# Token weights of a wave mixer flipped as bf16 instead of f32

## The chip, the cores and the metric

The kernel runs on one core of one Trainium2 chip. A core has a matrix engine (TensorE, PE in the profile; PEld is its weight load), three engines that work on 128 partitions by columns (VectorE = DVE, ScalarE = ACT, GpSimd = POOL) and SyncE (SP), which here only issues transfers. Each engine runs its own list of instructions strictly in order and waits on semaphores for the others. SBUF is the on-chip memory; PSUM, where TensorE writes, has eight banks of 2 KB per partition. The metric is device time in microseconds.

## What is computed

An attention with a decaying state, then a mixing network on its output:

```
for t in range(S):                       # r, k, v: [4, 8, 768, 48]
    cur = einsum('bhd,bhe->bhde', u * k_t, v_t)
    y_t = einsum('bhd,bhde->bhe', r_t, state + cur)
    state = w * state + einsum('bhd,bhe->bhde', k_t, v_t)
x = y as [4, 768, 384]                   # heads side by side
theta = x @ w_theta
zr, zi = x * cos(theta), x * sin(theta)
un = x + einsum('ts,bsd->btd', w_tok_r, zr) + einsum('ts,bsd->btd', w_tok_i, zi)
out = un + max(un @ w_ch, 0)
```

All inputs and the output are f32. The two token weights, `w_tok_r` and `w_tok_i`, are 768 x 768 and serve all four batches.

## The kernel before

The 768 positions of a batch are six chunks of 128, worked on in three pairs of chunks. For each batch, `heads` (line 487) scales r by powers of w (Rw, on POOL) and flips it (RT). For each pair, `attention` (line 506) loads k and v, scales k (Kw, POOL), flips it (KT), casts v (vb, ACT), computes scores (line 543), masks them (mAT, DVE, line 548), carries the state on (Sb), and sums the outputs in PSUM (lines 627 and 632). The diagonal term goes another way: PD (DVE), a small matmul, dg, yd (POOL). Then x is formed (DVE, line 639), flipped (xT), multiplied by w_theta (line 651), and sine and cosine (ACT, lines 655 and 658) lead to zi (POOL) and zr (DVE). `mixing` (line 668) needs zr and zi of all three pairs of a batch: for each of six row blocks, 12 matmuls of 128 x 384 (line 683) against WrT and WiT, then un (DVE), its flip (uT), the channel matmul (line 700), fin (DVE, line 704) and a store (SP, line 708). The mixing of one batch runs beside the attention of the next.

WrT and WiT are the token weights turned over, made once by `token_weights` (line 445): twelve row blocks of 128 x 768, each loaded in f32 into one of ten load buffers (`ld`, which k, v, w_theta and w_ch use in turn as well), turned over by six 128 x 128 transposes on TensorE against the f32 identity `ident_f`, and copied out of PSUM as bf16. All other flips go through `flips` (line 468), where the source is bf16 already, the identity is `ident`, and six or eight blocks fill one bank.

The order of all work is fixed when the kernel is built. Every piece is a task with the engines it may run on, an assumed cost on each, what it reads and writes, a priority, and the PSUM places it takes; `P.order()` (line 88) plays these costs through and writes each engine's list. PSUM is cut into six places, two of two banks and four of one (`SLOTS`, line 23); scores, score outputs, theta and channel sums take a double place, and so did a flipped row block of the token weights. Loads go out on SP in the order in which the program text asks for them, each when its buffer is free by the plan; stores go ahead of loads as soon as fin is ready by the plan (line 710). SP waits in order, so a load behind a store waits for what the store waits for. A task with several engines (`ev` at line 482: ACT or DVE) goes to the one that the plan finds free sooner. `lock=True` keeps the plan from running two such tasks at once: Rw, Kw, PD, yd and zi have it.

The change touches lines 445 to 466. Those of lines outside it that the text goes back to:

```
    Ls = ring(NL, [C, 2, H, Dp], F32, "ld")                      # ten load buffers
    load(3500 / parts, r_fs[b % NR][:, h], ...)                  # a batch's r: 1152 KB
    P.add({SP: (1000, 2000)}, ... out ..., prio=-2e6)            # the stores
```

Of the kernel before, what the change touches and what calls it, by code (L numbers as in the profile page):

```python
# [16 lines left out]
BF16 = mybir.dt.bfloat16  # L17
# [3 lines left out]
PE, DVE, ACT, POOL, SP = "PE", "DVE", "ACT", "POOL", "SP"  # L21
# [167 lines left out]
def act_op(n, psum=True, ptr=False):  # L189
    return (n / 1.2 + (85 if psum else 100) + (90 if ptr else 0), 135)  # L190


def dve_op(n, rate=1.0):
    return (n / (0.96 * rate) + 70, 115)


def pool_op(n, rate=1.8):
    return (170 + rate * n, 100)


def pe_op(ns):
    return (ns, 215)
# [24 lines left out]
def build(ctx, tc, nc, r, k, v, w, u, moe_w_theta, moe_w_tok_r, moe_w_tok_i, moe_w_ch, out):  # L227
    B, H, S, D = r.shape
    HD = H * D
    C = 128  # L230
    NCH = S // C
# [8 lines left out]
    P = Plan(SLOTS)  # L240
    banks = [ps.tile([C, n, 512], F32, name=f"bank{i}") for i, n in enumerate(SLOTS)]

    def dbl(tok):
        return banks[P.bank_of[tok]]
# [4 lines left out]
    def bank16(tok):  # L249
        return banks[P.bank_of[tok]].bitcast(BF16)[:, 0]  # L250

    def ring(n, shape, dt, nm):
        return [sb.tile(shape, dt, name=f"{nm}{i}") for i in range(n)]
# [3 lines left out]
    def copy(e, dst, src):  # L257
        if e == ACT:
            nc.scalar.activation(dst, src, Act.Copy)  # L259
        else:  # L260
            eng_of[e].tensor_copy(dst, src)  # L261

    ident_f = sb.tile([C, C], F32, name="ident_f")
    ident = sb.tile([C, C], BF16, name="ident")
# [18 lines left out]
    Ls = ring(NL, [C, 2, H, Dp], F32, "ld")  # L283
# [116 lines left out]
    def load(ns, dst, src, wr, pos=None):  # L400
        if pos is None:
            nload[0] += 1
            pos = nload[0]
        P.add({SP: (ns, 2100)}, lambda e: nc.sync.dma_start(out=dst, in_=src), wr=wr,  # L404
              prio=-1e6 + pos, name="load")
# [11 lines left out]
    def slot():  # L417
        nslot[0] += 1
        return nslot[0] % NL
# [9 lines left out]
    def flat(i):  # L429
        return Ls[i].rearrange("p a h d -> p (a h d)")  # L430

    def L2(i):
        return [("L", i, 0), ("L", i, 1)]
# [11 lines left out]
    def token_weights(tos, prio):  # L445
        for to in tos:
            for src, dst, key in ((moe_w_tok_r, WrT, "WrT"), (moe_w_tok_i, WiT, "WiT")):
                i = slot()
                load(1100, flat(i)[:, :S], src[to * C:(to + 1) * C, :], L2(i))
                tok = ("W", key, to)  # L450

                def flip(e, i=i, tok=tok):
                    for g in range(2):
                        for j in range(3):
                            o = (3 * g + j) * C
                            nc.tensor.matmul(dbl(tok)[:, g, j * C:(j + 1) * C],  # L456
                                             flat(i)[:, o:o + C], ident_f, is_transpose=True,
                                             start=(j == 0), stop=(j == 2))
                P.add({PE: pe_op(660)}, flip, rd=L2(i) + ["ident_f"], acq=[(tok, 2)],
                      prio=prio + to, name="Wflip")  # L460

                def evac(e, tok=tok, dst=dst, to=to):
                    copy(e, dst[:, :, to * C:(to + 1) * C].rearrange("p (g j) c -> p g j c", g=2),
                         dbl(tok)[:, :, :3 * C].rearrange("p g (j c) -> p g j c", j=3))
                P.add({ACT: act_op(6 * C), DVE: dve_op(6 * C)}, evac, use=[tok],
                      wr=[(key, to)], prio=prio + to, name="Wevac")

    def flips(dst, blocks, tok, prio, rd, wr, name, opts, src=lambda t: t):
        n = len(blocks)
# [12 lines left out]
    def ev(n):  # L482
        return {ACT: act_op(n), DVE: dve_op(n, 2.0)}
# [233 lines left out]
    attention(0, 1, 15)  # L717
    attention(0, 2, 25)
    token_weights(range(0, 3), 40)
    load_r(1)  # L720
    heads(1, 100)
    token_weights(range(3, NCH), 40)
    square(moe_w_ch, Wch, "Wch", 46)
    for b in range(1, B + 1):
# [39 lines left out]
```

## Time and profile before

| | |
|---|---|
| five runs | 158.66, 158.07, 158.57, 158.22, 161.15 us |
| median | 158.57 us |
| the profiled execution | 158.66 us, of which the span of its instructions is 156.8 us |
| TensorE busy | 131.9 us of the span |
| DVE, ACT, POOL busy | 110.2, 76.2, 75.6 us |
| moved by DMA | 25.0 MB |
| f32 flips of the token weights (line 456) | 72, from 29.9 to 48.3 us |
| copies out of them | 9 on ACT, 3 on DVE, from 30.9 to 49.1 us |
| first mixing matmul | 42.06 us |
| last load landed | 93.8 us |

Busy time of an engine is the union of its instructions. Matmuls overlap in the pipeline, so a group's mean duration is longer than its pace: 326 ns is the mean of a mixing matmul, and three of them move the chain on by 0.49 us. The chain of waits is read from the end backwards: each piece is the work or the transfer that the next piece waited for.

### The profile page before, as it was taken

The page shows a single profiled execution, that of the slowest core. Times are in us where ns is not written, and L with a number is a line of the kernel's source. Part 1 is how long each engine was busy: PE and PEld are TensorE (multiplying, and loading weights), DVE is VectorE, ACT ScalarE, POOL GpSimd, SP SyncE. Part 2 cuts the span into 40 slices and gives each one's busy share as a digit, 9 for nine tenths or more (in the row PEclk, how much of TensorE's full clock was granted, in tenths as well). Part 3 has the DMA queues.
Part 4 walks back from the last instruction along what each step waited for, and adds up shares of the span by engine and source line. Part 5 has one row for each costly group of instructions (what it writes and reads, how often), then busy time and mean ns, then how long its engine had stood idle before and what let it go on. Part 6 is the DMA issues. An engine that isn't in the chain of part 4 may idle for free.

```text
span 156.8 us, 3653 instructions
## 1 busy us (share of the span) xinstructions
PE 131.9 (84%) x1491; PEld 92.6 (59%) x1491; DVE 110.2 (70%) x158; ACT 76.2 (49%) x119; POOL 75.6 (48%) x61
## 2 busy tenths in 40 slices
PE   4077586569899999999989969999999999999950
PEld 1056464457687666668756737678567676566620
DVE  6296799840723989987999867658996975545540
ACT  3977228349887446648844365615418354000000
POOL 7000730759995755966599976900712343100000
PEclk9999999999999999999999999999999999999996
DMA  4999999999899999999999950311300022022022
GB/s 152 264 224 187 163 266 394 366 397 367 265 187 156 166 209 186 167 164 250 293 176 210 152 95 0 104 49 51 104 0 4 0 102 104 0 100 81 19 100 100
DMA packets 59962, 25.00 MB, mean 159 GB/s; under 512 B 50473, under 2 KB 58410, under 8 KB 59946
## 3 DMA queue, kind: packets, MB, share of 16 engines
q1 hardware_dynamic: 59920, 24.78, 74.1%
q8 instruction: 11, 0.18, 0.6%
q14 instruction: 5, 0.04, 0.1%
q10 hardware_dynamic: 26, 0.00, 0.0%
HBM read 20.06 MB, written 4.72 MB: 158 GB/s over the span
## 4 chain that ended last, share of the span: by engine, by line
PE 47%; DMA 18%; DVE 13%; SPq 8%; POOL 7%; issue 3%; ACT 2%; ACTq 1%; POOLq 0%; DVEq 0%
PE bank L683 20%; DMA ld<-in_k_dram 7%; SPq L404 7%; PE bank L473 7%; DMA r_f<-in_r_dram 7%; PE bank L700 7%; POOL Rw L492 4%; PE bank L651 3%; DMA ld<-in_v_dram 3%; PE bank L456 3%; POOL Kw L520 2%; DVE PD L553 2%; DVE fin L704 2%; DVE zr L661 2%; PE bank L543 2%
## 5 line engine op out<-in xcount | busy, mean ns | idle before, releaser
L683 PE MATMUL bank<-zi,WiT 128*128 128x384 bf16 x144 | 29.6, 326 | 0.0
L683 PE MATMUL bank<-zr,WrT 128*128 128x384 bf16 x144 | 29.1, 326 | 0.0
L548 DVE TENSOR_TENSOR mAT<-bank,mask 128x1024 bf16<-128x1024 f32 x24 | 28.7, 1215 | 0.1
L520 POOL TENSOR_TENSOR Kw<-ld,wpinv 128x768 bf16<-128x768 f32 x10 | 18.6, 1860 | 19.2 <-DMA ld<-in_k_dram 19.2
L664 POOL TENSOR_TENSOR zi<-x,sin 128x768 bf16<-128x768 bf16 x12 | 20.6, 1717 | 14.8 <-ACT sin L655 14.8
L568 POOL TENSOR_TENSOR yd<-dg,vb 128x768 bf16<-128x768 f32 x12 | 17.6, 1476 | 20.3 <-ACT dg L259 16.0
L689 DVE TENSOR_TENSOR un<-bank,x 128x384 bf16<-128x384 f32 x24 | 13.3, 552 | 6.7 <-PE bank L683 6.7
L492 POOL TENSOR_TENSOR Rw<-r_f,wpow 128x576 bf16<-128x576 f32 x12 | 16.6, 1405 | 2.9 <-DMA r_f<-in_r_dram 2.9
L683 PEld LDWEIGHTS <-WiT 128*128 128x128 bf16 x144 | 12.9, 98 | 7.1
L683 PEld LDWEIGHTS <-WrT 128*128 128x128 bf16 x144 | 12.8, 97 | 7.0
L259 ACT ACTIVATE vb<-ld 128x768 bf16<-128x768 f32 x12 | 10.1, 845 | 13.5 <-DMA ld<-in_v_dram 13.5
L639 DVE TENSOR_TENSOR x<-bank,yd 128x768 bf16<-128x768 f32 x12 | 11.4, 953 | 6.9 <-PE bank L632 4.8
L651 PE MATMUL bank<-Wth,xT 128*128 128x384 bf16 x72 | 13.7, 326 | 3.1 <-DVE xT L261 1.5
L704 DVE SCALAR_TENSOR_TENSOR fin<-bank,un 128x768 f32<-128x768 f32 x12 | 11.5, 956 | 6.3 <-PE bank L700 6.3
L259 ACT ACTIVATE RT<-bank 128x768 bf16<-128x768 bf16 x16 | 12.0, 814 | 5.4 <-PE bank L473 5.4
L655 ACT ACTIVATE sin<-bank 128x768 bf16<-128x768 f32 x12 | 9.7, 811 | 9.9 <-DVE fin L704 4.8
L700 PE MATMUL bank<-Wch,uT 128*128 128x384 bf16 x72 | 13.7, 326 | 0.7 <-DVE uT L261 0.7
L661 DVE TENSOR_TENSOR zr<-bank,x 128x768 bf16<-128x768 f32 x12 | 11.4, 950 | 3.0 <-ACT bank L658 3.0
L543 PE MATMUL bank<-RT,KT 64*128 64x128 bf16 x192 | 9.8, 229 | 2.1 <-ACT KT L259 0.6
L651 PEld LDWEIGHTS <-xT 128*128 128x128 bf16 x72 | 6.9, 97 | 7.9 <-DVE xT L261 1.9
L473 PE MATMUL bank<-ident,Rw 128*128 128x128 bf16 x96 | 8.3, 242 | 3.8 <-POOL Rw L492 2.0
L658 ACT ACTIVATE bank<-bank,pi 128x768 f32<-128x768 f32 x12 | 10.5, 873 | 0.0
(79 smaller groups left out, 209.8 us busy)
## 6 DMA issues: line engine op xcount, KB each, us to landing
ld<-in_k_dram SPq DMA_DIRECT2D x24, 192.0 KB, 5.7
ld<-in_v_dram SPq DMA_DIRECT2D x24, 192.0 KB, 5.3
out_dram<-fin SPq DMA_DIRECT2D x12, 384.0 KB, 2.5
r_f<-in_r_dram SPq DMA_DIRECT2D x3, 1152.0 KB, 10.1
ld<-in_moe_w_tok_r_dram SPq DMA_DIRECT2D x6, 384.0 KB, 7.5
ld<-in_moe_w_tok_i_dram SPq DMA_DIRECT2D x6, 384.0 KB, 8.5
r_f<-in_r_dram SPq DMA_DIRECT2D x2, 576.0 KB, 4.5
ld<-in_moe_w_theta_dram SPq DMA_DIRECT2D x1, 384.0 KB, 5.0
```

The lines of the kernel that those rows point to most:

```text
L259: nc.scalar.activation(dst, src, Act.Copy)
L473: nc.tensor.matmul(bank16(tok)[:, i * C:(i + 1) * C], s, ident, is_transpose=True, start=(i == 0), stop=(i == n - 1))
L492: eng_of[e].tensor_mul(Rw[:, :, 2 * hp:2 * hp + 2, :D].transpose([0, 2, 1, 3]), rf[:, 2 * hp:2 * hp + 2, :].rearrange("p h (n d) -> p h n ...
L520: eng_of[e].tensor_mul(Kw[:, :, :, :D].rearrange("p a h d -> p (a h) d"), Ls[ik][:, :, :, :D].rearrange("p a h d -> p (a h) d"), wpinv.rea ...
L548: P.add({DVE: dve_op(8 * C)}, lambda e, tk=tk, c=c: nc.vector.tensor_mul(mAT[:, c].rearrange("p a h t -> p (a h) t"), dbl(tk).rearrange("p ...
L568: P.add({POOL: pool_op(2 * HD, 1.7)}, lambda e: nc.gpsimd.tensor_mul(yd.rearrange("p a (h d) -> p (a h) d", h=H), wide(dg, D), vb.rearrang ...
L651: nc.tensor.matmul(dbl(th)[:, t, :HD], xT[:, ND * t + dk, :], Wth[:, dk, :], start=(dk == 0), stop=(dk == ND - 1))
L661: P.add({DVE: dve_op(2 * HD)}, lambda e: nc.vector.tensor_mul(zr[:, 2 * pr:2 * pr + 2], dbl(th)[:, :, :HD], x[:, 2 * pr:2 * pr + 2]), use= ...
L664: P.add({POOL: pool_op(2 * HD, 1.9)}, lambda e: nc.gpsimd.tensor_mul(zi[:, 2 * pr:2 * pr + 2], x[:, 2 * pr:2 * pr + 2], sn), rd=xk + [("si ...
L683: nc.tensor.matmul(bank(tm)[:, :HD], WT[:, so, to * C:(to + 1) * C], z[:, so], start=(part == 0 and j == 0), stop=(part == 3 and j == 2))
L700: nc.tensor.matmul(dbl(tf)[:, t, :HD], uT[:, ND * t + dk, :], Wch[:, dk, :], start=(dk == 0), stop=(dk == ND - 1))
L704: P.add({DVE: dve_op(2 * HD)}, lambda e: nc.vector.scalar_tensor_tensor(fin, dbl(tf)[:, :, :HD], 0.0, un, op0=Alu.max, op1=Alu.add), use=[ ...
```

## The change

The row block is cast to bf16 in its own load buffer, in two halves, each written over the first half of the bytes that it is read from. The planner may put this cast on ACT, DVE or POOL. The six transposes then read bf16 against the bf16 identity, and write bf16 into one bank instead of f32 into two; the copy out reads bf16 from one bank. The costs that the planner assumes change with it (660 to 340 ns for the flip).

```diff
-                def flip(e, i=i, tok=tok):
-                    for g in range(2):
-                        for j in range(3):
-                            o = (3 * g + j) * C
-                            nc.tensor.matmul(dbl(tok)[:, g, j * C:(j + 1) * C],
-                                             flat(i)[:, o:o + C], ident_f, is_transpose=True,
-                                             start=(j == 0), stop=(j == 2))
-                P.add({PE: pe_op(660)}, flip, rd=L2(i) + ["ident_f"], acq=[(tok, 2)],
+                half = Ls[i].bitcast(BF16).rearrange("p a h d -> p (a h d)")[:, :2 * S] \
+                    .rearrange("p (g c) -> p g c", g=2)[:, :, :S // 2]
+                P.add({ACT: act_op(S, False), DVE: dve_op(S, 2.0), POOL: pool_op(S, 1.1)},
+                      lambda e, i=i, half=half: copy(
+                          e, half, flat(i)[:, :S].rearrange("p (g c) -> p g c", g=2)), rd=L2(i), wr=L2(i),
+                      prio=prio + to, name="Wcast")
+
+                def flip(e, half=half, tok=tok):
+                    for j in range(NCH):
+                        nc.tensor.matmul(bank16(tok)[:, j * C:(j + 1) * C],
+                                         half[:, j // 3, (j % 3) * C:(j % 3 + 1) * C], ident, is_transpose=True,
+                                         start=(j == 0), stop=(j == NCH - 1))
+                P.add({PE: pe_op(340)}, flip, rd=L2(i) + ["ident"], acq=[(tok, 1)],
                       prio=prio + to, name="Wflip")
 
                 def evac(e, tok=tok, dst=dst, to=to):
-                    copy(e, dst[:, :, to * C:(to + 1) * C].rearrange("p (g j) c -> p g j c", g=2),
-                         dbl(tok)[:, :, :3 * C].rearrange("p g (j c) -> p g j c", j=3))
-                P.add({ACT: act_op(6 * C), DVE: dve_op(6 * C)}, evac, use=[tok],
-                      wr=[(key, to)], prio=prio + to, name="Wevac")
+                    copy(e, dst[:, :, to * C:(to + 1) * C],
+                         bank16(tok)[:, :S].rearrange("p (j c) -> p j c", j=NCH))
+                P.add(ev(S), evac, use=[tok], wr=[(key, to)], prio=prio + to, name="Wevac")
```

Since the plan is made anew from these tasks, instructions outside these lines move too, on every engine. The new cast has no `lock`.

## The prediction

> **What bounds the kernel now.** I read the slices first, then the chain that ended last, then the timeline of the engines where the chain turns from loads to TensorE.
>
> ```profile
> PE   4077586569899999999989969999999999999950
> PEclk9999999999999999999999999999999999999996
> DMA  4999999999899999999999950311300022022022
> GB/s 152 264 224 187 163 266 394 366 397 367 265 187 156 166 209 186 167 164 250 293 176 210 152 95 0 104 49 51 104 0 4 0 102 104 0 100 81 19 100 100
> ```
>
> A slice is 3.92 us. Loads run without a pause until 93 us: near 380 GB/s from 24 to 41 us (token weights and two loads of r, long rows), near 163 GB/s while k and v come in. Then they stop and TensorE works alone, with its clock full, so no term below needs a clock. The two stages meet here:
>
> ```profile
> 82.51 1.47 SPq L404
> 83.98 0.05 issue
> 84.03 4.96 DMA ld<-in_v_dram
> 89.09 0.06 ACT vb L259
> 89.16 0.81 issue
> 89.96 0.81 ACT sin L655
> 90.77 0.78 ACT bank L658
> 91.57 0.96 DVE zr L661
> 92.53 0.47 DVE xT L261
> 93.05 1.15 PE bank L651 x6
> ```
>
> A v load lands, ACT casts it (vb) and only then reaches the sine and cosine queued behind; zr, xT and theta (L651) follow. TensorE waited 1.53 us for that theta. From the last score output of batch 2 (L627 and L632, 94.69) to TensorE's end (152.29) are 57.6 us. The work queued there, by the chain's pieces (three mixing matmuls 0.49, six theta or channel matmuls 0.97, six flips 0.34): 180 mixing 29.3, thirteen theta and channel groups 12.6, sixteen flip groups 5.4, batch 3's attention 7.6, these outputs 0.7; together 55.6. So the end is this meeting point plus TensorE's remaining work, and the loads set the meeting point.
>
> **Flips: -4.1 us of TensorE.** The chain gives 12 f32 flips 1.33 to 1.40 us, 0.113 each; bf16 flips take 0.34 for six, 0.057 each. 72 of them: 8.2 becomes 4.1. Six of the twelve groups (4.1 us in f32) stand between the first mixing matmul (42.06) and 49.4, when 21 mixing matmuls are done (3.4); in the new order all flips stand before the first.
>
> **Copies out: -1.8 us off the path.** Before, nine on ACT at 0.81 and three on DVE at 0.958: 10.2. After, the planner places seven on ACT (0.81, as for bf16 xT) and five on DVE (0.547, as for xT): 8.4. Both engines have idle time there, so this counts as nothing by itself; without that cover it is 1.8 us.
>
> **Casts: twelve new instructions.** The planner puts four on ACT, six on DVE, two on POOL. ACT: 0.845, the row of vb (same shape and types). DVE:
>
> ```profile
> L345 DVE CAST ident<-ident_f 128x128 bf16<-128x128 f32 x1 | 0.2, 220 | 0.0
> L261 DVE COPY xT<-bank 128x768 bf16<-128x768 bf16 x6 | 3.3, 547 | 0.0
> L261 DVE CAST WrT<-bank 128x768 bf16<-128x768 f32 x2 | 1.9, 958 | 3.1 <-PE bank L456 3.1
> ```
>
> Between 0.55 and 0.96. ident's cast is the same kind: 220 ns for 128 columns, less 0.15 for the fixed part (dg, 16 columns, takes 165), is 0.55 ns a column, about xT's pace (0.52) and half that of the f32 copy out (1.05). I take 0.55. POOL: between a fill of that size (0.74) and a product (1.48); I take 1.3.
>
> **Where the casts wait.** DVE's casts read and write SBUF while POOL works nearly without a break. The only DVE operation of the page with every operand in SBUF that runs beside POOL's products is PD:
>
> ```profile
> 56.66 1.82 POOL L520 TENSOR_TENSOR Kw<-ld,wpinv 128x768 bf16<-128x768 f32 x1 [1.60 <-DMA ld<-in_k_dram]
> 57.52 1.50 DVE L553 TENSOR_TENSOR PD<-RT,KT 128x1024 bf16<-128x1024 bf16 x1
> 33.21 2.77 POOL L492 TENSOR_TENSOR Rw<-r_f,wpow 128x576 bf16<-128x576 f32 x2 [2.91 <-DMA r_f<-in_r_dram]
> ```
>
> PD takes 0.68 alone, 1.50 here: it got through when POOL's product ended. A zi just behind another PD took 2.09 for 1.64. PD has two inputs, a cast one, so the wait is zero at the one end and the rest of a POOL instruction at the other. I take the upper end, by the nearest row.
>
> The Trainium skill ("SBUF — State Buffer", Who interferes with whom) speaks against the change here: a copy or cast in a two-port mode takes the port pair that DVE shares with GpSimd, and the second to come is blocked until the first has finished. No row here shows it for a one-input cast; by that rule the upper end is the sum, without it the lower.
>
> **Walk to the first mixing.** Landings follow from bytes in the queue's order at the moved rate, plus 1 to 2 us (this gives 33.1 for the r load, where the trace has 33.12). ACT's two casts of r's row blocks, the second waiting for its landing near 26.3, and a copy-out now stand ahead of the table load: cosine of the first pair ends 30.85 instead of 28.22. zr follows at 31.8 (before 29.9), the second half of the third pair's scores and its mask at 34.1 (before 31.49); zr now stands ahead of x, so x of the third pair ends 37.65 (before 34.5). POOL's two casts hold up one yd by 1.6 (28.7 to 30.3), hidden behind that late x. Then DVE's last four casts alternate with POOL's Rw and zi, each waiting for the one in front: 38.8, 40.75, 42.7, 44.9, with xT and three copies between. A last copy and zr end at 46.4. Mixing starts at 46.6 instead of 42.06, but with no flips left: 21 matmuls later it is 50.0 against 49.4, **+0.6**. Without the blocking the same sequence gives 43.3 and 46.7, -2.7. The flips' 4.1 us are thus spent before they reach the path.
>
> **A load changes places.** On SP the second whole load of r (r_f, 1152 KB, for batch 2) stood at 31.23; now it stands behind the first store, which waits for fin. POOL's four Rw for it (41.88 to 47.39) leave the place ahead of the first Kw of batch 1 and come between zi and yd of that batch instead, where POOL idles (page: yd waits 20.3 us in all), so I count them at nothing; ahead of a late yd they would cost their 5.5. k and v of batch 1 gain: their bytes end at 52.9 instead of 56.5 (r's 3.1 us at 380 GB/s, and 0.5 of a gap). But SP's queue then stops at the store until fin:
>
> ```profile
> 31.23 0.43 SPq L404 DMA_DIRECT2D r_f<-in_r_dram  x1
> 54.77 1.08 SPq L404 DMA_DIRECT2D ld<-in_k_dram  x1
> 56.31 0.72 SPq L708 DMA_DIRECT2D out_dram<-fin  x1
> 57.12 1.34 SPq L404 DMA_DIRECT2D ld<-in_k_dram  x1
> ```
>
> fin keeps its distance of 6.9 us behind the 49.4 mark (56.28), so it ends at 56.6 (bounds 53.6 to 57.5). Behind the store stand r_f and all 24 loads of batches 2 and 3. Bytes restart about 1.2 us after issue (the first load: issued 0.80, moving after 2.0), at 57.9; store 1.2, r 3.1, one k load 1.2 make 63.4, where 59.0 stood before: the stream is late by about 4, by 1.5 at the lower bound. It ran at its 163 GB/s with waits of about 0.1 us at the other stores, so nothing catches up.
>
> **The meeting point.** The last v landed at 93.82; now 97.8. In ACT's new order its cast comes ahead of the sine of batch 2's first pair (before, behind it). Cast, sine, cosine and zr took 3.55 in that place (93.82 to 97.36), and the last score output waits for the PSUM pair which that zr frees: 101.35 instead of 94.69. In exchange TensorE has done more: 27 mixing matmuls (4.4) and one flip group (0.34) have moved ahead of that output, 4.75 in all. 101.35 - 94.69 - 4.75 = **+1.9**. TensorE itself would arrive there at about 97.7 (with a wait for vb's neighbours 99.6), so the load decides. On the profiled execution (158.66, span 156.8, 1.86 outside) this is 160.6; the median is 158.57, 0.09 below, so **160.5**.
>
> **Rivals.**
> *The casts do not block* (one input, unlike PD). The start of mixing gains 2.7, fin ends at 53.6, the stream is late by 1.5, the last v lands at 95.3, the output starts at 98.85: -0.6, 158.0. For it: PD is a product, not a cast. Against: ident's pace, twice that of the f32 copies, asks for a wider read of SBUF than they have.
> *The loads are not what TensorE waits for*: k and v waited for buffers, not for bytes, and they catch up behind the store. Then TensorE's arrival counts: 95.0 without blocking, 97.7 with it, so -4.4 to -1.7; I take the middle, -3.1, 155.5. For it: POOL and ACT also wait often for each other, and flips are 4.1 us of work that is gone. Against: the DMA row of nines.
> *DVE becomes the bound behind the meeting point*: it is busy 9.95 of the 10 us from 110 to 120, and with PD and the copies of batch 2 pushed behind the masks it loses 2 to 3 more (two PD at 0.68 and a copy at 0.69 that come later): 1.9 + 2.5, 163.0. It decides as soon as the output starts after 102.
> *The cast runs at the slow pace*: six times 0.4 without blocking, 2.4 before mixing; fin near 56, as in the forecast; 160.2, counted with it.
>
> **Chances.** Forecast 0.45, no blocking 0.20, loads not deciding 0.25, DVE 0.10. A measurement of this kernel can tell 0.3%, 0.48 us, from no change. The second rival is faster; half of the first is; the rest of it is mostly no change. Faster 0.34, same 0.12, slower 0.54. The forecast alone spans 159.2 to 162 (fin's bounds); reaching into the rivals on both sides, 155.6 to 163.0.
>
> **What would show it.** Right: DVE casts of 1.0 to 1.9 us beside POOL; first mixing near 46.6; the second whole r load issued at 56 to 58 with idle DMA before it; a wait of ACT for a v load at 96 to 99, TensorE idle 2 us or more there. Wrong: casts of 0.55 throughout; the first mixing before 44; the last v at 94 or earlier. If the last v lands late and TensorE does not wait, the step from landing to PSUM pair is wrong.

## The result, and the profile after

The changed kernel takes 160.63 us, the median of 22 runs (158.78 to 163.74); the kernel before took 158.75 on the same chips (43 runs). The ratio is 1.010, with a 95% interval of 1.0074 to 1.0126: it became 1% slower. Of most kernels here some executions are more than 1.5% slower than the fastest of the same kernel; ratios and intervals, here and below, leave these out, while the medians hold all, so the quotient of two medians is not the ratio. The profiled execution below took 162.07 us (span 160.4), above its median, so marks read from it lie up to about 1.5 us late; the same holds of two experiments, the kernel before with three stores moved (160.16 profiled, median 157.52) and with r moved (165.20 profiled, median 162.91).

The 40 slices of the changed kernel (4.01 us each) are:

```profile
PE   4077686593889999994979899999999999999950
PEclk9999999969789999999599999999999999999997
DMA  4999999999999239999999994005200020221122
GB/s 156 258 231 178 163 293 393 372 394 299 152 169 150 46 108 299 179 157 241 181 335 182 174 165 59 4 0 196 97 7 4 0 98 4 98 98 54 44 98 98
```

Against the row of before there is now a hole in DMA at 52 to 60 us (2 and 3 tenths), and TensorE dips at 36 to 40 and at 72 to 76 (3 and 4 tenths). Loading ends one slice later, near 98 us. The clock, full throughout before, falls three times.

SP's queue explains the hole:

```profile
48.15 3.04 SPq L404 DMA_DIRECT2D ld<-in_v_dram  x2
56.93 0.39 SPq L712 DMA_DIRECT2D out_dram<-fin  x1
57.37 1.88 SPq L404 DMA_DIRECT2D r_f<-in_r_dram  x1
59.34 2.32 SPq L404 DMA_DIRECT2D ld<-in_k_dram  x2
```

From 51.2 to 56.9 SP issues nothing: it stands at the first store, whose fin ends at 56.90. Batch 2's r and all k and v of two batches stand behind it; before, r went out at 31.23 and SP issued loads until 55.85.

Next the engines' timeline while the token weights are turned over (start, duration, engine, line, operation, output and input):

```profile
36.20 1.80 DVE L261 CAST ld<-ld 128x768 bf16<-128x768 f32 x1
37.55 4.76 POOL L496 TENSOR_TENSOR Rw<-r_f,wpow 128x576 bf16<-128x576 f32 x3
39.66 1.38 DVE L261 CAST ld<-ld 128x768 bf16<-128x768 f32 x1
41.43 1.29 DVE L261 CAST ld<-ld 128x768 bf16<-128x768 f32 x1
43.11 0.54 DVE L261 CAST ld<-ld 128x768 bf16<-128x768 f32 x1
44.55 1.64 POOL L668 TENSOR_TENSOR zi<-x,sin 128x768 bf16<-128x768 bf16 x1 [2.25 <-ACT sin L659]
44.80 1.81 DVE L261 CAST ld<-ld 128x768 bf16<-128x768 f32 x1
46.66 0.51 PE L461 MATMUL bank<-ident,ld 128*128 128x128 bf16 x6 [0.76 <-DVE ld L261]
```

The cast at 43.11 ran in POOL's only gap (42.31 to 44.55) and took 0.54. Its neighbours, the same instruction beside a POOL product, took 1.29 to 1.81. TensorE waited for them; the page's row of the flips, out of 6.6 us busy, has 4.3 us of idle time put down to the cast:

```profile
L461 PE MATMUL bank<-ident,ld 128*128 128x128 bf16 x72 | 6.6, 241 | 5.3 <-DVE ld L261 4.3
```

The first mixing matmul starts at 47.34. Last, where loads and TensorE meet; first ACT's timeline, then the chain of waits (start, duration, what):

```profile
70.88 0.84 ACT L259 ACTIVATE vb<-ld 128x768 bf16<-128x768 f32 x1 [5.64 <-DMA ld<-in_v_dram]
71.63 0.79 ACT L659 ACTIVATE sin<-bank 128x768 bf16<-128x768 f32 x1
...
94.27 0.84 ACT L259 ACTIVATE vb<-ld 128x768 bf16<-128x768 f32 x1 [2.16 <-DMA ld<-in_v_dram]
99.33 0.84 ACT L259 ACTIVATE vb<-ld 128x768 bf16<-128x768 f32 x1
```

```profile
64.82 5.98 DMA ld<-in_v_dram
70.81 0.03 ACTq L259
70.83 0.04 issue
70.88 0.06 ACT vb L259
70.94 0.69 issue
71.63 0.67 ACT sin L659
72.29 0.03 issue
72.32 0.88 ACT bank L662
73.19 0.02 issue
73.22 0.96 DVE zr L665
```

The v that ACT waits 5.64 us for is the first v behind the held store, not the last. Its cast stands ahead of the sine of batch 1's second pair, zr waits for that, and TensorE runs nearly dry: it is busy 1.71 of the 4 us from 72 to 76. Behind the first mixing the chain holds one load of k or v, this one; from there TensorE, DVE and ACT carry the lateness to the last score output of batch 2, at 103.03 (94.52 before, both at the first of the two groups). SP turned to this v at 61.79; the chain follows it back to 64.82 only, and what held its second half in between stays open.

### The profile page after: what moved, and what is told of

Its sections match the earlier page's. It is cut to its first block, busy times and chain, and to the rows that moved or that the text cites. A ratio compares the mean times of both kernels' runs of the same rounds, so it can differ in the third digit from the quotient of the medians.

```text
span 160.4 us, 3675 instructions
## 1 busy us (share of the span) xinstructions
PE 132.7 (83%) x1491; PEld 91.7 (57%) x1491; DVE 119.9 (75%) x171; ACT 74.5 (46%) x115; POOL 76.9 (48%) x63
## 4 chain that ended last, share of the span: by engine, by line
PE 58%; DMA 14%; SPq 12%; DVE 9%; issue 2%; ACT 2%; DVEq 0%; ACTq 0%
PE bank L687 27%; SPq L404 12%; PE bank L477 8%; PE bank L704 7%; DMA ld<-in_moe_w_tok_r_dram 6%; PE bank L655 6%; DMA ld<-in_moe_w_tok_i_dram 4%; DMA ld<-in_v_dram 4%; PE bank L547 3%; DVE ld L261 2%; DVE zr L665 2%; PE bank L636 2%; PE bank L589 1%; DVE PD L557 1%; PE bank L461 1%
## 5 line engine op out<-in xcount | busy, mean ns | idle before, releaser
L687 PE MATMUL bank<-zi,WiT 128*128 128x384 bf16 x144 | 29.0, 326 | 0.0
L668 POOL TENSOR_TENSOR zi<-x,sin 128x768 bf16<-128x768 bf16 x12 | 19.7, 1640 | 18.1 <-ACT sin L659 18.0
L496 POOL TENSOR_TENSOR Rw<-r_f,wpow 128x576 bf16<-128x576 f32 x12 | 17.2, 1463 | 0.8 <-PE bank L547 0.8
L655 PE MATMUL bank<-Wth,xT 128*128 128x384 bf16 x72 | 15.5, 358 | 0.3 <-ACT xT L259 0.3
L704 PE MATMUL bank<-Wch,uT 128*128 128x384 bf16 x72 | 14.3, 337 | 1.3 <-DVE uT L261 1.3
L477 PE MATMUL bank<-ident,Rw 128*128 128x128 bf16 x96 | 9.4, 255 | 2.6 <-DVE Rw L496 1.8
L461 PE MATMUL bank<-ident,ld 128*128 128x128 bf16 x72 | 6.6, 241 | 5.3 <-DVE ld L261 4.3
```

The source lines that it names most:

```text
L477: nc.tensor.matmul(bank16(tok)[:, i * C:(i + 1) * C], s, ident, is_transpose=True, start=(i == 0), stop=(i == n - 1))
L496: eng_of[e].tensor_mul(Rw[:, :, 2 * hp:2 * hp + 2, :D].transpose([0, 2, 1, 3]), rf[:, 2 * hp:2 * hp + 2, :].rearrange("p h (n d) -> p h n ...
L655: nc.tensor.matmul(dbl(th)[:, t, :HD], xT[:, ND * t + dk, :], Wth[:, dk, :], start=(dk == 0), stop=(dk == ND - 1))
L668: P.add({POOL: pool_op(2 * HD, 1.9)}, lambda e: nc.gpsimd.tensor_mul(zi[:, 2 * pr:2 * pr + 2], x[:, 2 * pr:2 * pr + 2], sn), rd=xk + [("si ...
L687: nc.tensor.matmul(bank(tm)[:, :HD], WT[:, so, to * C:(to + 1) * C], z[:, so], start=(part == 0 and j == 0), stop=(part == 3 and j == 2))
L704: nc.tensor.matmul(dbl(tf)[:, t, :HD], uT[:, ND * t + dk, :], Wch[:, dk, :], start=(dk == 0), stop=(dk == ND - 1))
```

## The experiments

Three marks sort all of them: the first mixing matmul, the issue of the first store, and the last score output of batch 2 (called y here). Except for one run with a lock, only the order of the planned list was edited, or an engine in it, after the planner had run. In the diffs `out0` is the first store, `r2.0` batch 2's r load, `v6.1` the second v load of batch 2's first pair, `r3.0`, `v9.1` and `v10.1` the same of batch 3 (its r, its first and its second pair), `WrT5` the last row block of w_tok_r, `vb6` the cast of batch 2's first v, `cos4` the cosine of batch 1's second pair, `zi3` the zi of its first, `rs2` batch 2's Rw; a pair means that the first is put right behind the second.

| run | base | median, us | ratio to before | first mixing | first store | r of batch 2 | y | span |
|---|---|---|---|---|---|---|---|---|
| before | | 158.57 | 1 | 42.06 | 56.31 | 31.23 | 94.52 | 156.8 |
| after | | 160.63 | 1.010 [1.0074, 1.0126] | 47.34 | 56.93 | 57.37 | 103.03 | 160.4 |
| e1_r_early | after | 159.45 | 1.0017 [0.9981, 1.0054] | 46.64 | 57.50 | 28.87 | 100.50 | 157.8 |
| e2_store_late | after | 158.46 | 0.9896 [0.9781, 1.0012] | 46.43 | 58.75 | 50.77 | 99.19 | 156.5 |
| e3_v_behind_sine | after | 161.97 | 1.010 [1.0039, 1.0161] | 45.74 | 55.32 | 55.76 | 101.75 | 159.1 |
| e4_casts_act | after | 160.30 | 1.0111 [1.005, 1.0172] | 45.95 | 55.54 | 55.98 | 100.33 | 157.7 |
| e9_casts_pool | after | 159.60 | 1.005 [0.9997, 1.0103] | 44.65 | 54.23 | 54.67 | 100.61 | 157.9 |
| e6_act_store | after | 158.11 | 0.9967 [0.9929, 1.0004] | 45.35 | 59.97 | 51.21 | 97.99 | 155.3 |
| e7_lock | after | 160.84 | none | 41.19 | 58.45 | 51.00 | 100.95 | 157.8 |
| e10_after_stores_late | after | 157.80 | 0.9925 [0.9881, 0.997] | 46.41 | 60.32 | 51.00 | 99.04 | 156.4 |
| e11_pool_stores_late | after | 156.67 | 0.9833 [0.9785, 0.9881] | 44.91 | 59.62 | 51.08 | 97.54 | 154.9 |
| e8_before_stores_late | before | 157.52 | 0.9882 [0.9828, 0.9936] | 44.12 | 60.94 | 32.61 | 96.13 | 158.4 |
| e5_before_r_late | before | 162.91 | 1.0167 [1.0036, 1.0299] | 43.68 | 59.11 | 59.59 | 101.17 | 163.5 |
| e12_before_r_rw_late | before | 164.90 | 1.0368 [1.028, 1.0456] | 42.95 | 58.34 | 58.78 | 100.95 | 163.3 |

Medians come from three groups of runs, with the kernel before at 159.22 (e1, e2, e3, e5), 159.95 (e4, e6, e7, e9) and 159.98 (e8, e10, e11, e12) beside them, so ratios are what compares; marks and span are one profiled execution each. For the lock run no ratio is on record.

One regularity needs no theory: the span ends 57.3 us after y (57.25 to 57.4) in the changed kernel and in e1, e2, e3, e4, e6, e9, e10 and e11, whether y is at 98 or at 103; in the four rows with the order of before it ends 62.3 after y (the lock run, planned anew, 56.9). So nearly everything that differs from run to run with the same order happens before y, and the planner's new order had done 5.0 us more of TensorE's work by then.

The chains of waits sort the runs too. Behind the first mixing, those of e1, e2, e6, e10 and e11 hold no load of k or v; those of the changed kernel, e4 and e9 hold one, the first v behind the held store; in e3 and e7 it is a later v, in e5 the first v and a later one. The chain of before holds a k and a v, that of e8 none, that of e12 a k.

**r moved ahead of the store.**

```diff
+    for one, other in [('r2.0', 'WrT5')]:
+        t = ts.pop(at(one))
+        ts.insert(at(other) + 1, t)
```

> The changed kernel with one transfer moved: batch 2's load of r goes out on SP right after the sixth row block of w_tok_r, where it stood before the change. All else keeps its place. Theory A (the store holds r and all later loads back; a v cast that waits for its load stands ahead of a sine on ACT, and TensorE stalls there): first store still issued near 57, no DMA pause ahead of it longer than 1 us, the 5.6 us wait of ACT for v near 65 shrinks to under 2.5, time 157 to 158.5, that is 2 to 3.5 below the changed kernel's 160.6. Rival B (what the blocked casts lose at the start is the whole loss, the loads are hidden): 160.6 within 0.5. Rival C (the new order on DVE and TensorE after 75 us sets the end): 160 or more, the wait on ACT gone all the same.

Ratio 1.0017, against 1.010: the loss is gone, though Theory A had asked for more (157 to 158.5; it took 159.45). The store still stops SP until 57.5, but r is in. The 5.64 us wait of ACT is gone. Later v loads still keep ACT waiting 1.41 and 3.73 us, but they are not in the chain.

**The first store moved behind batch 2's first k and v.**

```diff
+    for one, other in [('out0', 'v6.1')]:
```

> The changed kernel with one transfer moved: the first store goes out on SP behind batch 2's first k and v, so that r, k and v no longer wait for fin. Theory A: r is issued near 51 instead of 57, the v that ACT waited for until 70.9 lands near 66, time 156.5 to 158.5. Rival B and rival C: 160.6 within 0.6.

Ratio 0.9896: 2 points under the changed kernel, from moving one transfer of 384 KB. The first v no longer makes ACT wait; its cast starts here, without a wait, instead of at 70.88:

```profile
64.21 0.84 ACT L264 ACTIVATE vb<-ld 128x768 bf16<-128x768 f32 x1
```

The waits left are 1.04, 2.77 and 0.39 us, outside the chain.

**Is it ACT's order?** The cast of that v is put behind the sine and cosine that waited behind it.

```diff
+    for one, other in [('vb6', 'cos4')]:
```

> The changed kernel with one instruction moved: on ACT the cast of batch 2's first v goes behind the sine and cosine of batch 1's second pair, which it stood ahead of. No load moves. Theory A: that sine starts near 69.5 instead of 71.6, TensorE's gaps from 72 to 82 shrink, time 158.5 to 160 (1 to 2 below the changed kernel). Rivals B and C: 160.6 within 0.5.

Sine starts at 67.97 instead of 71.63, and nothing is gained: 1.010 again, which Rivals B and C had said and Theory A had not. ACT now waits 0.82, 4.05 and 4.48 us for the later v loads, and the chain runs through one of them (landed at 88.3), issued on SP behind the third store. So the place of one cast chooses which load is waited for. That the late stream is the cause rests on the two runs above.

**The load move alone, in the kernel before.**

```diff
+    for one, other in [('r2.0', 'out0')]:
```

> The kernel before with one transfer moved: batch 2's load of r goes out on SP directly behind the first store, as in the changed kernel; flips, casts and all orders on the engines as before. Theory A: k and v of batch 1 land 3 earlier, k and v of batch 2 land 2.5 to 4 later, ACT waits for v ahead of a sine near 70, time 160 to 161.5 (1.5 to 3 above 158.5). Rival B: 158.5 within 0.5, since no cast blocks. Rival C: 158.5 within 0.5.

Here POOL scales batch 2's r before it is loaded, so that batch's r is not the reference's; the amount of work is the same. Ratio 1.0167, as Theory A had it: moving r behind the store costs by itself about as much as the whole change. The interval, 0.4 to 3.0%, is wide. The first v behind the store is in its chain too (61.61, 8.32 us long).

**The casts off DVE**, on ACT and, in another run, on POOL.

```diff
+        if t.name == "Wcast" and t.eng == DVE:
+            t.eng = ACT        # POOL in e9_casts_pool
```

> The changed kernel with DVE's six casts given to ACT, each at its place in the planned order; nothing else moves. Theory A (each cast on DVE waits for a POOL product, so mixing starts late, fin is late, the store and all loads behind it are late): DVE's chain ahead of mixing loses 8.6 us of cast time and waiting, ACT gets 6 x 0.85; first mixing matmul near 45 instead of 47.5, first store near 54.5 instead of 57, time 157.5 to 159.3. Rival D (the blocking at the start is hidden, only the store's place counts): first mixing earlier, but time 160.2 or more.

> The changed kernel with DVE's six casts given to POOL, each at its place in the planned order. POOL's own two took 0.83 and 0.88. No operation of DVE then meets POOL between 28 and 46 us, at the price of 6 x 0.85 in POOL's list. Theory A: POOL's products and casts take turns as before (0.85 in place of 0.55 each), so zi of the last pair comes near 44, first mixing 45 to 47, time 158.5 to 160.3. Rival D: 160.2 or more whatever the start.

Mixing starts 1.4 and 2.7 us earlier than in the profile of the changed kernel, and the store goes out that much earlier too. That profile is a late one: against e3, where the casts are on DVE and the stores in place as well (mixing 45.74, store 55.32), ACT gains nothing and POOL 1.1 us. The times hardly answer: 1.0111 on ACT, no gain; 1.005 on POOL, half a per cent, with intervals that overlap. ACT still waits for v loads, 4.24, 2.59 and 3.69 us in the one, 4.29, 3.06 and 4.06 in the other. A gain like the one forecast for the absence of blocking does not appear.

**Casts on ACT and the store late.** Both edits above together.

> Both repairs at once: the six DVE casts on ACT, and the first store behind batch 2's first k and v. Theory A: the two share one path (late fin, late stream), so they add only in part: 155.5 to 157.5, below the kernel before (158.5). Rival B (the start alone): the same as with the casts on ACT alone. Rival D: the same as with the store moved alone, 157.0 (ratio 0.99).

Ratio 0.9967, y at 97.99. Theory A had expected the two edits to add in part; the run ranks with the late store alone (the intervals overlap), so nothing shows ACT, which then is busy all 8 us from 38 to 46, to be a better place for the casts.

**A lock on the cast**, so that the planner keeps it from running beside POOL's products, and makes its plan anew.

```diff
-                      prio=prio + to, name="Wcast")
+                      prio=prio + to, lock=True, name="Wcast")
```

> The changed kernel with lock=True on the cast, so that the planner keeps it from running beside POOL's products; the whole plan is made anew. In the new order batch 2's load of r stands directly ahead of the first store instead of behind it. Theory A: no DVE cast above 0.9 us, r issued before fin, time 156 to 158.5. Rival C (the new orders after 75 us are worse whatever the start): 160 or more.

160.84 us (158.89 to 161.74, four runs), where Theory A expected 156 to 158.5; 160 or more was what Rival C gave, but with a whole new order the run can't tell the theories apart. r did go out ahead of fin, at 51.00. The plan's separation of casts and products does not survive on the chip; DVE's timeline, and the POOL product beside it:

```profile
42.63 3.25 DVE L262 CAST ld<-ld 128x768 bf16<-128x768 f32 x2
...
42.38 3.08 POOL L497 TENSOR_TENSOR Rw<-r_f,wpow 128x576 bf16<-128x576 f32 x2
```

Two casts took 3.25 us, until Rw was through. Mixing began at 41.19 but with flips among its matmuls, and the first flip of Kw behind it came at 51.70 (50.76 after the change).

**Three stores late, in the changed kernel, with the casts on POOL as well, and in the kernel before.**

```diff
+    for one, other in [('out0', 'v6.1'), ('out1', 'r3.0'), ('out2', 'v9.1')]:      # e10, e11
+    for one, other in [('out0', 'v6.1'), ('out1', 'v9.1'), ('out2', 'v10.1')]:     # e8
```

> The changed kernel with the first three stores moved back: the first behind the first k and v of batch 2 (as in the earlier run with one store moved), the second behind the r of batch 3, the third behind the next k and v. Theory A: the later stores hold the stream too (in the run with the first store moved alone, the second held the queue from 64.6 to 68.5), so the last score output of batch 2 starts earlier than the 99.2 of that run, near 97, and the span ends 57.3 us after it: span 154 to 156, time 155.5 to 157.5, ratio 0.975 to 0.99. Rival 1 (only the first store and the r behind it matter, the buffers hold the rest): as that run, near 158.4, ratio 0.99 to 1.0. Rival 2 (moved stores hold back fin's two buffers and so DVE and the mixing): slower than that run, 159 or more.

> The same three stores moved back, and DVE's six casts on POOL, where a cast took 0.83 to 0.88 us and DVE could not be held by it. Theory A with blocking as a second cost: the mixing starts at 44.7 as in the run with the casts on POOL alone, 2 us ahead of the run beside it; with no store in the way the earlier fin buys no loading, so at most 0.5 us more than the run beside it: 155 to 157, ratio 0.975 to 0.985. Rival (blocking at the start is worth its whole 2 us once the stores are out of the way): 153.5 to 155, ratio 0.965 to 0.975. Rival (the start is hidden wholly): equal to the run beside it.

> The kernel before, with its first three stores moved back in SP's queue: the first behind the first k and v of batch 2, the second behind batch 3's r and its first k and v, the third behind the next k and v. Theory A (what a store that waits for fin holds back in SP's queue comes late at the meeting point, and nothing else of the queue matters): the kernel before loses only about 0.5 us of loading at its first store, where its second whole r was already in, so little is to be had: 157.8 to 158.8 on a chip where the kernel before takes 158.6, ratio 0.995 to 1.000. Rival (the stores hold the loads in the kernel before as much as after the change, and moving them back helps any order): 156 to 157, ratio 0.985 to 0.99.

With three stores moved (0.9925) the changed kernel does no better than with one (0.9896), and y is the same within 0.15 us: Theory A's second part, that the later stores hold the stream too, falls for the changed kernel. In the chain of this run no load of k or v is left; from the first mixing on it is TensorE, with DVE and one copy on ACT in between. And now it counts where the casts run. The run with the casts on POOL starts mixing 1.50 us earlier, has y 1.50 us earlier and a span 1.5 us shorter; the medians, taken side by side, are 157.80 and 156.67, the ratios 0.9 points apart. The rival's whole 2 us did not come, nor Theory A's 0.5 at most. The move takes the casts' own time off DVE as well, so it is not blocking alone. And whether it is worth more here than with the stores early (0.5 points) stays open: both differences are uncertain by 0.6 points or more. POOL's casts there, among the same Rw:

```profile
38.32 1.58 POOL L269 CAST ld<-ld 128x768 bf16<-128x768 f32 x2
39.87 1.40 POOL L504 TENSOR_TENSOR Rw<-r_f,wpow 128x576 bf16<-128x576 f32 x1
41.22 0.82 POOL L269 CAST ld<-ld 128x768 bf16<-128x768 f32 x1
```

and DVE's in the run beside it:

```profile
38.42 1.38 DVE L266 CAST ld<-ld 128x768 bf16<-128x768 f32 x1
40.19 1.29 DVE L266 CAST ld<-ld 128x768 bf16<-128x768 f32 x1
```

The kernel before gains from late stores too, 0.9882, where Theory A expected 0.995 to 1.000; the rival's 0.985 to 0.99 is what came. The theory had looked at how long SP stands still at a store, some 0.5 us. The chain of waits of before says more; these pieces lead up to the ones that the prediction showed:

```profile
77.71 0.95 DVE fin L704
78.66 0.86 DVE zr L661
79.53 0.47 DVE Sb L613
80.00 1.10 SPq L708
81.10 0.05 issue
81.15 0.02 SPq L404
```

The load that set the meeting point of before had itself come through the third store, issued at 78.76. With the stores moved, no load issued after the first ones (a k at 9.88) is left in this chain either.

**The load move in the kernel before, with POOL's Rw moved behind it.**

```diff
+    for one, other in [('r2.0', 'out0'), ('rs2.0', 'zi3'), ('rs2.1', 'rs2.0'), ('rs2.2', 'rs2.1'), ('rs2.3', 'rs2.2')]:
```

> The kernel before (f32 flips, no casts), with the whole r of batch 2 loaded behind the first store, and POOL's four products Rw of it moved behind the zi of batch 1's first pair, so that they read the new r. Theory A: this move alone makes the loss of the changed kernel: the stream restarts late by about 3 us behind the store, the meeting point moves, and with the f32 flips not saved the time is 160 to 162, ratio 1.01 to 1.02; the run in which Rw was left in its place gave 1.017 [1.004, 1.030]. Rival (r's place is hidden and the casts made the loss): 158.2 to 159.2, ratio 0.998 to 1.003.

1.0368, far above Theory A's 1.01 to 1.02. POOL's timeline, then DVE's:

```profile
70.90 5.49 POOL L497 TENSOR_TENSOR Rw<-r_f,wpow 128x576 bf16<-128x576 f32 x4
76.34 1.48 POOL L573 TENSOR_TENSOR yd<-dg,vb 128x768 bf16<-128x768 f32 x1
...
77.86 0.96 DVE L644 TENSOR_TENSOR x<-bank,yd 128x768 bf16<-128x768 f32 x1 [3.47 <-POOL yd L573]
```

All four Rw stand in one block ahead of a yd, and x waits 3.47 us for it. In the changed kernel three of them ran at 65.85 and the last at 75.53, behind yd (74.09), with no such wait. The run thus measures two costs at once, and the one without the Rw move stays the better measure of the load's.

## Why the prediction was right, step by step

The time of 160.5 us met 160.63, and the cause is the one forecast: a load that has slid behind a store. That the two agree within 0.2 us is in part luck. The wait was not where it was put, and two sizes behind it were off in opposite directions.

- **Flips.** At full clock six bf16 flips take 0.33 to 0.34 us in the chain, as counted. Some ran at about half clock, 0.65 for six. That the saving is spent before the path holds: with three late stores in both kernels, the changed one stands at 0.9925 [0.9881, 0.997] and the old one at 0.9882 [0.9828, 0.9936], so even without held loads the change gains nothing that shows.
- **Copies out.** Seven on ACT at 0.81 to 0.83, five on DVE at 0.54 to 0.56: as counted. One of DVE's stands in the chain all the same, between the flips at 43.58 and the last cast, where the prediction counted the copies at nothing.
- **Casts.** ACT 0.83 to 0.87, DVE 0.54 when undisturbed: right. POOL was mis-sized: 0.83 and 0.88 measured, 1.3 taken (1.13 at most, once, in the run with all of DVE's casts there).
- **Blocking.** The upper end was right: five of DVE's six casts took 1.29 to 1.81. The rule of the Trainium skill ("SBUF — State Buffer", Who interferes with whom), which the rows of before did not show for one input, is shown here by 0.54 beside 1.29 to 1.81. The first mixing came at 47.34 (46.6 forecast; 45.7 to 46.6 in e1, e2, e3 and e10, which have the same casts). Twenty-one matmuls later it is 50.76 (50.0).
- **What blocking is worth.** The first rival put its absence at 2.5 us of the end. With the casts on POOL the runs give 0.5 points (0.8 us) while the stores hold the loads; once they don't, 1.5 us in the marks and 1.1 in the medians. The step that failed there is that an earlier fin brings the whole stream forward: with the casts on POOL the store went out 2.7 us earlier than in the changed kernel's profile, but the k and v loads still kept ACT waiting 4.29, 3.06 and 4.06 us.
- **The load that changes places.** fin ended at 56.90 and r was issued at 57.37 with DMA idle before it, where 56.6 and 56 to 58 were forecast. (By the prediction's own terms, 50.0 and 6.9 us, the sum is 56.9 and not 56.6.) SP had issued its last load at 95.67, 5.3 us later than before (90.38), where the stream was put about 4 late. Three runs carry this step: moving r back ahead is worth 0.8 points, moving the store back 2.0, and moving r behind the store in the kernel before costs 1.7.
- **The meeting point.** y less the start of the last v's cast is 3.70 us (3.34 to 3.70 over e1, e2, e3, e6 and e9; 3.55 forecast). But it is 3.70 in e10 and e11 too, where no load is in the chain, so this distance doesn't show that a load set y. The work done ahead of y is worth 5.0 us (4.75). In the chain, y starts at 103.20 in an execution that is 1.4 us above the median, where 101.35 was forecast. But ACT's wait of 96 to 99 did not come: the last v was cast at 99.33 without a wait, and TensorE, forecast to idle 2 us or more there, was busy from 92 to 102 throughout. So by the prediction's own sign its step from the last landing to the PSUM pair is wrong. TensorE ran dry at 72 to 76 instead: the lateness entered at the first v behind the store (a 5.64 us wait), and was carried on. The step "ahead of a sine" was right in kind, but I looked for it only at the last pair.
- **TensorE's own arrival.** Put at 97.7; with no load in its way it arrived at 99.04, from nearly the same first mixing (46.41, and 46.6 in the forecast). From first mixing to y it takes 52.6 us there and in the run with the casts on POOL, not 51.1. So held loads were worth 1.8 points of the time (1.010 against 0.9925) or 2.8 us, where the steps made it 3.65: TensorE's part was 1.3 too small, the loads' part 0.9 too large. Of the 1.8, 1.2 were in the kernel before as well (0.9882 with its stores late).
- **The clock.** The prediction put it at nothing. In the chain, behind the wait for the load, a channel group, six flips and a theta group (75.84 to 80.52) took 1.76, 0.65 and 1.38 us where e10 has 1.15, 0.35 and 1.15 at the same place: 1.1 us in this execution, which is a late one. How much of the loss this is over all executions was not separated. The clock alone does not order the times: over the six executions of e11 its mean went from 0.948 to 0.984, and the one at 0.984 was the slowest.
- **The rivals.** "The loads are not what TensorE waits for" falls with e1, e2 and e5. "DVE becomes the bound" from an output later than 102 falls with the profile itself: y was at 103.03, and the end 57.4 after it, as in the run with y at 97.99.
- **A reading that was missed.** The prediction counted 0.1 us of waiting at the second and third store of before. The chain of before ran through the third one, and moving three stores is worth 1.2% there. Which of the three matters, and by its data or by its issue, was not tried and stays open.

One version beats both kernels, the changed one with its three stores late and the casts on POOL: 156.67 us (156.53 to 157.08), ratio 0.9833 [0.9785, 0.9881]. The kernel before with late stores alone had 157.24 at its lowest; the intervals of the two ratios overlap.

## What to carry to other kernels

When a change makes a planner order the work anew, read the queues first: a load that has slid behind a store costs what the store waits for, and it can outweigh everything that the edit itself does. A cast from SBUF to SBUF on VectorE is priced with the GpSimd instruction beside it, or tried on GpSimd. And a sum that comes out doesn't prove its steps: here only the runs with one transfer moved told where the wait was.

## What the runs showed of the hardware that was not expected

The prediction said that the clock is full and no term needs one. In some stretches after TensorE had been little busy, the clock granted to it fell to about half for some 4 us. In windows of 2 us, first of the changed kernel, then of the run with r and Rw moved in the kernel before (columns: window, its length, busy time of PE, PEld, DVE, ACT and POOL, then the clock, DMA share and GB/s):

```profile
38.00:40.00 2.00, 0.72 (x10) 0.55 (x11) 2.00 (x4) 1.39 (x2) 2.00 (x2) 1.00 1.32 233
40.00:42.00 2.00, 1.20 (x20) 0.97 (x18) 2.00 (x3) 0.51 (x2) 2.00 (x2) 1.00 0.65 113
42.00:44.00 2.00, 2.00 (x12) 1.26 (x11) 1.65 (x3) 0.79 (x2) 0.30 (x1) 0.53 1.19 188
44.00:46.00 2.00, 1.90 (x21) 1.73 (x18) 1.68 (x2) 1.97 (x3) 1.45 (x1) 0.62 1.40 163
```

```profile
68.00:70.00 2.00, 0.32 (x8) 0.24 (x9) 1.93 (x3) 0.15 (x1) 2.00 (x2) 1.00 1.49 172
70.00:72.00 2.00, 0.56 (x4) 0.36 (x4) 0.00 (x0) 2.00 (x4) 2.00 (x2) 1.00 1.26 148
72.00:74.00 2.00, 2.00 (x10) 1.04 (x9) 0.58 (x1) 0.17 (x1) 2.00 (x3) 0.65 0.91 152
74.00:76.00 2.00, 2.00 (x8) 0.91 (x6) 0.38 (x1) 0.61 (x1) 2.00 (x2) 0.50 0.98 171
```

In the 4 us before the fall TensorE was not idle: it was busy 1.92 of 4 in the one and 0.88 in the other, and then had work at about half clock. No share of busy time comes out as the limit: after 1.34 of 4 from 36 to 40 in the changed kernel the clock stayed at 1.00 for 2 us more, after 2.27 of 4 from 28 to 32 it was 0.50. The Trainium skill ("TensorE: Matmul & The Clock Gate", What's actually happening) states that the clock falls to half after an idle window of about 3.4 us; the runs agree in the half, but show it with TensorE partly busy. It is not the change's alone: the kernel before with late stores had a clock of 0.52 at 26 to 28 us, after 0.79 of 2 us busy, while the profiled execution of before had 1.00 there.

GpSimd casts 128 x 768 from f32 to bf16 in 0.82 to 0.88 us (once 1.13), little more than half the time of its product of that size (1.48), and so faster than VectorE's cast beside such a product.
